# Gated loads in groups, and layer 1 of one stripe chunk by chunk, in a fused attention and feed-forward kernel

## The chip, the cores and the metric

The kernel runs on one core of a Trainium2 chip. The metric is device time in microseconds (us) of one execution, as a median over executions. All times compared here are of the fast state of the machine, unless a run is said to be slow.

Engines: TensorE (PE in the profile; PEld are its weight loads), VectorE (DVE), ScalarE (ACT), GpSimd (POOL) and SyncE (SP, whose queue issues most DMA). An engine waits for the others by semaphores. In this kernel the program order on each engine is the order in which the Python code emits the work.

## The reference, cut to what matters

The inputs q, k and v have shape (4, 8, 768, 64). A decayed causal linear attention gives 3072 tokens of width 512, which go through a feed-forward layer of width 2048.

```python
# attention: in blocks, with a running state per head
intra = (q_b k_b^T * Dmask) v_b
inter = (q_b * lam_pow) @ kv_state
kv_state = lam_block * kv_state + (k_b * rev_pow)^T v_b
# feed-forward ("smelu" is a smooth ReLU)
h = x @ w_in                       # 3072 x 512 @ 512 x 2048
g = where(h >= 1, h, where(h <= -1, 0, (h + 1)**2 / 4))
out = g @ w_out                    # 2048 x 512
```

## The kernel before: the parts that matter

Tokens come in 24 chunks of 128. Four chunks make a stripe of 512 tokens; there are six stripes. A chunk has two units `u` (half of the heads each), and a unit has three steps:

- `t`: transpose q (`pq`), multiply k by [v, identity] (`pk`); ScalarE copies `pq` to `qbd` and half of `pk` to `kT`; VectorE adds the other half to the state `U`.
- `s`: scores `ps`, masked by VectorE into `sc`.
- `o`: output `po` from `U` and `sc`; ScalarE copies it to `xT`, the input of layer 1.

`cast` scales q and k to bf16 (GpSimd, in the first stripe k by VectorE) and casts v into `vi` (ScalarE). `l1(s, i)` and `l2(s, i)` are steps of layer 1 and layer 2 of stripe `s`, 16 each, four 512-column matmuls per step.

```python
def l1(s, ni):
    ph = pp_h.tile([128, MS], F32, name="ph", tag="ph")
    for ko in range(KO):
        nc.tensor.matmul(ph, lhsT=w_in_sb[:, ko, ni * 128:(ni + 1) * 128], rhs=xT[s][:, ko, :],
                         start=(ko == 0), stop=(ko == KO - 1))
    # ... ScalarE: r = relu(ph + 1); every second step VectorE's three SmeLU instructions t, w, gT

# prologue: attention of stripe 0, weights started from chunk 1 on
ensure_loaded(CPS - 1)                       # CPS = 4
for c in range(CPS):
    ensure_cast(c, nc.vector)
    if c >= 1:
        load_w_in(state["wi"]); state["wi"] += 1
    for _ in range(4):                       # t(u) | s(u) ; o(u-1) comes behind t(u)
        a, b_ = att_step()
        for f in a + b_: f()
load_w_in(state["wi"])
for i in range(WS): load_w_out(i)
ensure_loaded(CPS + 1); ensure_cast(CPS)
# ... one att_step; ensure_loaded(CPS + PF)  with PF = 5

# main loop: in each of 16 steps of a stripe
#   l1(s, i) ; t or s of attention further on ; smelu(s, i) ; l2(s - 1, i) ; o of attention
```

So t always stands before the o of the unit ahead, t and s of one unit are a whole step (l1 and l2) apart, and attention of stripe 1 is spread over layer 1 of stripe 0.

## Time and profile before

The median is 263.86 us (263.35 to 263.87, 3 runs). The profiled execution spans 263.5 us.

| stretch, us | what happens | TensorE busy |
|---|---|---|
| 0 to 28.5 | attention of stripe 0 | 14.85 of 28.5 |
| 28.5 to 41.5 | nearly nothing: waits for chunk 4's v | 0.47 of 13 |
| 41.5 to 79 | attention of stripe 1 and layer 1 of stripe 0 | 28.08 of 37.5 |
| 79 to 240 | layer 1, layer 2 and attention mixed | 160.06 of 161 |

First the page of the kernel before: busy time by engine, then the span in 40 equal slices of 6.6 us. A digit is a busy share in tenths; PEclk is the granted TensorE clock in tenths.

```profile
span 263.5 us, 3576 instructions
PE 222.8 (85%) x1209; PEld 118.7 (45%) x1232; DVE 143.8 (55%) x245; ACT 173.7 (66%) x389; POOL 54.2 (21%) x61
...
PE   0567306666889999999999999999999999999993
...
PEclk9999755999999999999999999999999999999998
```

The stretches of the table, from the view by windows (length, busy time of each engine with its count, granted clock, DMA share, GB/s):

```profile
core 0: us, PE busy (x) PEld busy (x) DVE busy (x) ACT busy (x) POOL busy (x), PEclk, DMA share, GB/s
0.00:28.50 28.50, 14.85 (x72) 8.19 (x73) 13.53 (x28) 18.90 (x46) 12.56 (x22) 0.96 1.08 188
28.50:41.50 13.00, 0.47 (x4) 0.26 (x2) 0.74 (x2) 1.10 (x3) 1.04 (x1) 0.63 1.22 196
41.50:79.00 37.50, 28.08 (x159) 15.29 (x162) 26.21 (x39) 29.77 (x71) 15.75 (x14) 0.93 1.22 217
79.00:240.00 161.00, 160.06 (x892) 86.30 (x908) 99.17 (x172) 118.58 (x262) 24.87 (x24) 1.00 0.31 74
```

The hole at 28.5 us in the view of waits (28 to 42 us): TensorE waits for ScalarE's v cast, and that cast for a DMA. The eight weight loads had been issued by then and shared the DMA engines, which moved 196 GB/s all through the hole.

```profile
PE pk L173 <- ACT vi_152 L158: 12.6, 1, 12.6
ACT vi_152 L158 <- DMA vf<-in_v_dram: 11.9, 1, 11.9
```

### The profile page before, as it was taken

What the parts mean: (1) busy time and instruction counts of PE and PEld (TensorE: products, weight loads), DVE (VectorE), ACT (ScalarE), POOL (GpSimd) and SP (SyncE); (2) the same over time, 40 slices, a digit from 0 to 9 for tenths busy, and PEclk for the clock granted to TensorE, in tenths of its full rate; (3) what the DMA queues carried; (4) which work ended last, traced back from release to release, by engine and by line L of the source; (5) the groups of instructions that cost most, each with busy time, mean ns of one, the idle gap of its engine ahead of it and who ended that gap; (6) DMA issues with size and microseconds to landing.
All of it is one profiled execution on the core that took longest, in us unless ns stands there. A gap on an engine that the chain in (4) does not pass through costs nothing.

```text
span 263.5 us, 3576 instructions
## 1 busy us (share of the span) xinstructions
PE 222.8 (85%) x1209; PEld 118.7 (45%) x1232; DVE 143.8 (55%) x245; ACT 173.7 (66%) x389; POOL 54.2 (21%) x61
## 2 busy tenths in 40 slices
PE   0567306666889999999999999999999999999993
PEld 0234203333445555555555555555555544444441
DVE  3554201388887576657574766574747645555300
ACT  4768303778996977797779777977796754554210
POOL 3418111552340332033303320333000000000000
PEclk9999755999999999999999999999999999999998
DMA  6999999999990526753574357110111011111122
GB/s 134 210 217 187 196 196 220 210 226 218 218 202 2 138 67 120 159 128 85 108 159 121 88 113 163 40 40 0 42 41 40 2 40 40 40 42 40 40 80 80
DMA packets 82721, 29.58 MB, mean 112 GB/s; under 512 B 75536, under 2 KB 79632, under 8 KB 82704
## 3 DMA queue, kind: packets, MB, share of 16 engines
q1 hardware_dynamic: 78480, 25.18, 45.5%
q0 software_dynamic: 4224, 4.19, 9.7%
q8 instruction: 9, 0.15, 0.3%
q14 instruction: 8, 0.07, 0.1%
HBM read 27.27 MB, written 6.29 MB: 127 GB/s over the span
## 4 chain that ended last, share of the span: by engine, by line
PE 69%; DVE 3%; ACT 1%; issue 0%; ACTq 0%
PE py L258 31%; PE ph L234 26%; PE po L207 3%; PE ps L192 3%; PE pk L173 2%; PE po L206 2%; PE pq L169 1%; DVE gT L250 1%; DVE w_726 L249 1%; DVE sc L195 0%; DVE w_768 L249 0%; ACT r L238 0%; DVE U L186 0%; ACT xT L212 0%; ACT osb L262 0%
## 5 line engine op out<-in xcount | busy, mean ns | idle before, releaser
L234 PE MATMUL ph<-xT,w_in_sb 128*128 128x512 bf16 x380 | 99.6, 383 | 1.7 <-ACT r L238 1.3
L238 ACT ACTIVATE r<-ph,one 128x512 bf16<-128x512 f32 x96 | 65.9, 687 | 43.3 <-PE ph L234 39.6
L258 PE MATMUL py<-w_out_sb,gT 128*128 128x512 bf16 x365 | 92.3, 379 | 1.0
L234 PEld LDWEIGHTS <-w_in_sb 128*128 128x128 bf16 x384 | 37.9, 99 | 37.6 <-issue 2.8
L258 PEld LDWEIGHTS <-gT 128*128 128x128 bf16 x384 | 37.6, 98 | 32.3
L153 POOL TENSOR_TENSOR qs<-qf,tab_q 128x512 bf16<-128x512 f32 x24 | 25.3, 1052 | 121.7 <-PE pq L169 92.0
L186 DVE TENSOR_TENSOR U<-pk,U 128x256 bf16<-128x256 f32 x32 | 13.6, 424 | 56.5 <-ACT kT L179 56.5
L212 ACT CAST xT<-po 64x256 bf16<-64x256 f32 x96 | 35.3, 367 | 4.5 <-PE po L207 3.7
L195 DVE TENSOR_TENSOR sc<-ps,causal 128x512 bf16<-128x512 f32 x48 | 32.9, 685 | 4.6 <-PE ps L192 4.0
L156 POOL TENSOR_TENSOR ks<-kf,tab_k 128x512 bf16<-128x512 f32 x20 | 22.3, 1117 | 7.9 <-DMA kf<-in_k_dram 7.9
L262 ACT COPY osb<-py 128x512 f32<-128x512 f32 x24 | 14.2, 591 | 12.4 <-PE py L258 12.4
L169 PE MATMUL pq<-ident,qs 128*128 128x128 bf16 x96 | 14.3, 235 | 6.7 <-POOL qs L153 6.7
L179 ACT CAST kT<-pk 128x256 bf16<-128x256 f32 x48 | 17.9, 372 | 2.4 <-PE pk L173 1.3
L173 PE MATMUL pk<-vi_152,ks 128*128 128x256 bf16 x32 | 6.8, 298 | 14.6 <-ACT vi_152 L158 12.6
L169 PEld LDWEIGHTS <-qs 128*128 128x128 bf16 x96 | 10.1, 106 | 16.8 <-POOL qs L153 6.7
L173 PEld LDWEIGHTS <-ks 128*128 128x128 bf16 x96 | 8.1, 103 | 20.5 <-issue 8.1
L192 PEld LDWEIGHTS <-kT 128*128 128x128 bf16 x96 | 8.5, 101 | 19.4 <-ACT kT L179 11.0
L158 ACT CAST vi_152<-vf 128x512 bf16<-128x512 f32 x8 | 4.9, 610 | 11.9 <-DMA vf<-in_v_dram 11.9
L177 ACT COPY qbd_146<-pq 64x256 bf16<-64x256 bf16 x32 | 11.6, 361 | 1.6 <-PE pq L169 1.2
L177 ACT COPY qbd_144<-pq 64x256 bf16<-64x256 bf16 x32 | 11.5, 361 | 0.6 <-PE pq L169 0.2
L177 ACT COPY qbd_148<-pq 64x256 bf16<-64x256 bf16 x32 | 11.5, 361 | 0.5
L206 PEld LDWEIGHTS <-U 128*128 128x128 bf16 x80 | 8.2, 102 | 7.8 <-issue 3.7
(187 smaller groups left out, 213.9 us busy)
## 6 DMA issues: line engine op xcount, KB each, us to landing
qf<-in_q_dram SPq DMA_DIRECT2D x24, 256.0 KB, 4.8
kf<-in_k_dram SPq DMA_DIRECT2D x24, 256.0 KB, 4.7
vf<-in_v_dram SPq DMA_DIRECT2D x24, 256.0 KB, 5.0
out_dram<-osb SPq DMA_DIRECT2D x24, 256.0 KB, 2.0
w_in_sb<-in_moe_w_in_dram POOLq DMA_DIRECT2D x4, 512.0 KB, 8.7
w_out_sb<-in_moe_w_out_dram POOLq DMA_DIRECT2D x4, 512.0 KB, 15.5
lam_b<-in_lam_dram SPq DMA_DIRECT2D x1, 4.0 KB, 2.9
```

Source lines behind the costliest of these rows:

```text
L153: nc.gpsimd.tensor_tensor(t, qf, _bc(tab_q[:, cb, :], 2, D), op=AX.mult)
L156: k_eng.tensor_tensor(t, kf, _bc(tab_k[:, cb, :], 2, D), op=AX.mult)
L169: nc.tensor.transpose(out=pq[:, j, :], in_=qs[c][:, 2 * hp:2 * hp + 2, :].rearrange("p a d -> p (a d)"), identity=ident)
L173: nc.tensor.matmul(pk[:, j], lhsT=ks[c][:, 2 * hp:2 * hp + 2, :].rearrange("p a d -> p (a d)"), rhs=vi[c % NV][:, hp], start=True, stop=True)
L177: nc.scalar.copy(out=qb[hi * 64:hi * 64 + 64, :, hi, :], in_=pq[hi * 64:hi * 64 + 64])
L179: nc.scalar.copy(out=t, in_=pk[:, :, 1, :])
L192: nc.tensor.matmul(ps[:, 2 * j:2 * j + 2, :], lhsT=kT[u][:, j, :], rhs=qbd[u % NQ][:, j], start=True, stop=True)
L195: nc.vector.tensor_tensor(t, ps, _bc(causal, 1, 4), op=AX.mult)
L212: nc.scalar.copy(out=xT[st][hi * 64:hi * 64 + 64, 2 * hf:2 * hf + 2, off:off + C], in_=po[hi * 64:hi * 64 + 64, :, hi, :])
L234: nc.tensor.matmul(ph, lhsT=w_in_sb[:, ko, ni * 128:(ni + 1) * 128], rhs=xT[s][:, ko, :], start=(ko == 0), stop=(ko == KO - 1))
L238: nc.scalar.activation(out=r_t[s][:, ni % 2, :], in_=ph, func=AF.Relu, bias=one[:, 0:1])
L258: nc.tensor.matmul(py, lhsT=gT[s][:, ko, ms * 128:(ms + 1) * 128], rhs=w_out_sb[:, ko, :], start=(ko == 0), stop=(ko == FO - 1))
```

## The change

The intent: bring in the data strictly in the order in which it is needed, so that no weight delays a token chunk that is needed earlier, and give TensorE work from layer 1 of stripe 1 (a quarter as soon as a chunk is done) while layer 2 still lacks its weights. In `items`, the first `t` of a chunk now stands behind the last `o` of the chunk ahead, where it stood before it. The diff, cut to its core:

```diff
-    def load(c):
+    def load(c, after=None):          # the first DMA of the chunk waits for the DMA `after`
...
+    nc.scalar.preload_act_table_set("natural_log_exp_and_others")
-    nc.sync.dma_start(out=lam_b, ...)
+    nc.scalar.dma_start(out=lam_b, ...)
-    NV = 3                            # and qkp bufs 3
+    NV = 4                            # and qkp bufs 4
...
+    def l1(s, ni, n, part):           # n = 1: as before; n = 4: 4 x 4 matmuls of 128 columns,
+        ...                           # one quarter (one chunk) of the stripe, 4 row blocks of w_in
...
+    items = []
+    for u in range(NU):
+        if u % 2 == 0 and u > 0:
+            items += [("o", u - 1), ("t", u)]        # next chunk only after the last o
+        else:
+            items += [("t", u)] + ([("o", u - 1)] if u > 0 else [])
+        items.append(("s", u))
...
+    load_to(CPS - 1)
+    for c in range(CPS):
+        cast_to(c)
+        if c == CPS - 1:
+            for i in range(WS):
+                load_w_in(i)
+            load_to(CPS, after=w_dma[2])
+            load_to(2 * CPS - 1)
+        att_to(done(c))
+    run(zip_(l1s(0, 1, 0), []), 0)                   # layer 1 of stripe 0, alone
+    att_to(done(CPS))                                # chunk 4, alone
+    for c in range(CPS + 1, 2 * CPS):                # chunks 5, 6, 7, each with a quarter
+        run(zip_(l1s(1, CPS, c - CPS - 1), []), done(c) - st["it"])
+    for i in range(WS):
+        load_w_out(i)
+    load_to(2 * CPS, after=w_dma[WS + 2])
+    load_to(2 * CPS + LD - 1)
+    st["ahead"] = True
+    run(zip_(l1s(1, CPS, CPS - 1), []), 0)           # the last quarter
+    run(zip_([], l2s(0)), done(3 * CPS - 1) - st["it"])     # layer 2 of stripe 0 with attention
+    for s in range(2, NST + 1):                      # l1, items, smelu, l2, items: spread evenly
+        a = done(min((s + 2) * CPS, NCH) - 1)
+        run(zip_(l1s(s, 1, 0) if s < NST else [], l2s(s - 1)), a - st["it"])
```

More of the change, by code (lines that the diff above doesn't have):

```diff
@@ L55 @@
     NU = NCH * 2
+    LD = 6
     const = ctx.enter_context(tc.tile_pool(name="const", bufs=1))
     big = ctx.enter_context(tc.tile_pool(name="big", bufs=1))
-    ld = ctx.enter_context(tc.tile_pool(name="ld", bufs=6))
-    qkp = ctx.enter_context(tc.tile_pool(name="qkp", bufs=3))
+    ld = ctx.enter_context(tc.tile_pool(name="ld", bufs=LD))
+    qkp = ctx.enter_context(tc.tile_pool(name="qkp", bufs=4))
     ktp = ctx.enter_context(tc.tile_pool(name="ktp", bufs=3))
@@ L79 @@
     qkv_ld = {}
-    def load(c):
+    w_dma = []
+    SYNC = mybir.DependencyInfo(mybir.DependencyClass.Sync, mybir.DependencyReason.DATA)
+    def load(c, after=None):
         b, s0 = c // NCB, (c % NCB) * C
@@ L85, in load @@
             t = ld.tile([128, H, D], F32, name=f"{name}f", tag=f"{name}f")
-            nc.sync.dma_start(out=t, in_=src[b, :, s0:s0 + C, :].rearrange("h p d -> p h d"))
+            d = nc.sync.dma_start(out=t, in_=src[b, :, s0:s0 + C, :].rearrange("h p d -> p h d"))
+            if after is not None:
+                tc.add_manual_dep(d.ins, after.ins.name, SYNC)
+                after = None
             ts.append(t)
         qkv_ld[c] = ts
+    nc.scalar.preload_act_table_set("natural_log_exp_and_others")
     lam_b = const.tile([128, H], F32)
-    nc.sync.dma_start(out=lam_b, in_=lam.partition_broadcast(128))
+    nc.scalar.dma_start(out=lam_b, in_=lam.partition_broadcast(128))
     load(0)
@@ L139, in load_w_in, with cast @@
         n = d_ff // WS
-        nc.gpsimd.dma_start(out=w_in_sb[:, :, i * n:(i + 1) * n], in_=w_in_r[:, :, i * n:(i + 1) * n])
+        w_dma.append(nc.gpsimd.dma_start(out=w_in_sb[:, :, i * n:(i + 1) * n],
+                                         in_=w_in_r[:, :, i * n:(i + 1) * n]))
     def load_w_out(i):
         n = FO // WS
-        nc.gpsimd.dma_start(out=w_out_sb[:, i * n:(i + 1) * n, :], in_=w_out_r[:, i * n:(i + 1) * n, :])
+        w_dma.append(nc.gpsimd.dma_start(out=w_out_sb[:, i * n:(i + 1) * n, :],
+                                         in_=w_out_r[:, i * n:(i + 1) * n, :]))
     qs, ks = {}, {}
-    def cast(c, k_eng):
+    def cast(c):
         qf, kf, vf = qkv_ld.pop(c)
@@ L155, in cast @@
         t = qkp.tile([128, H, D], BF16, name="ks", tag="ks")
-        k_eng.tensor_tensor(t, kf, _bc(tab_k[:, cb, :], 2, D), op=AX.mult)
+        (nc.vector if c < CPS else nc.gpsimd).tensor_tensor(t, kf, _bc(tab_k[:, cb, :], 2, D), op=AX.mult)
         ks[c] = t
@@ L200, in stage_o @@
         cb = c % NCB
-        st, off = c // CPS, (c % CPS) * C
+        sx, off = c // CPS, (c % CPS) * C
         po = pp_o.tile([128, 2, 2, 128], F32, name="po", tag="po")
@@ L208, in stage_o, with smelu @@
                              start=(cb == 0), stop=True)
-        if st not in xT:
-            xT[st] = xp.tile([128, KO, MS], BF16, name="xT", tag="xT")
+        if sx not in xT:
+            xT[sx] = xp.tile([128, KO, MS], BF16, name="xT", tag="xT")
         for hi in range(2):
-            nc.scalar.copy(out=xT[st][hi * 64:hi * 64 + 64, 2 * hf:2 * hf + 2, off:off + C],
+            nc.scalar.copy(out=xT[sx][hi * 64:hi * 64 + 64, 2 * hf:2 * hf + 2, off:off + C],
                            in_=po[hi * 64:hi * 64 + 64, :, hi, :])
-    def att(i):
-        u, odd = i // 2, i % 2
-        a, b_ = [], []
-        if not odd:
-            if u < NU:
-                a.append(lambda: stage_t(u))
-            if 1 <= u <= NU:
-                b_.append(lambda: stage_o(u - 1))
-        elif u < NU:
-            a.append(lambda: stage_s(u))
-        return a, b_
     gT, r_t, py_t = {}, {}, {}
-    def l1(s, ni):
+    def l1(s, ni, n, part):
         ph = pp_h.tile([128, MS], F32, name="ph", tag="ph")
-        for ko in range(KO):
-            nc.tensor.matmul(ph, lhsT=w_in_sb[:, ko, ni * 128:(ni + 1) * 128], rhs=xT[s][:, ko, :],
-                             start=(ko == 0), stop=(ko == KO - 1))
-        if ni % 2 == 0:
+        m = MS // n
+        for j in range(n):
+            for ko in range(KO):
+                nc.tensor.matmul(ph[:, j * m:(j + 1) * m],
+                                 lhsT=w_in_sb[:, ko, (ni + j) * 128:(ni + j + 1) * 128],
+                                 rhs=xT[s][:, ko, part * m:(part + 1) * m],
+                                 start=(ko == 0), stop=(ko == KO - 1))
+        i = (ni // n) % 2
+        if i == 0:
             r_t[s] = rp.tile([128, 2, MS], BF16, name="r", tag="r")
-        nc.scalar.activation(out=r_t[s][:, ni % 2, :], in_=ph, func=AF.Relu, bias=one[:, 0:1])
-    def smelu(s, ni):
-        if ni % 2 == 0:
+        nc.scalar.activation(out=r_t[s][:, i, :], in_=ph, func=AF.Relu, bias=one[:, 0:1])
+    def smelu(s, ni, n, part):
+        if (ni // n) % 2 == 0:
             return
+        m = MS // n
         r = r_t[s]
-        if ni == 1:
+        if s not in gT:
             gT[s] = gp.tile([128, FO, MS], BF16, name="gT", tag="gT")
@@ L249, in smelu @@
         nc.vector.tensor_tensor(w, r, t, op=AX.subtract)
-        nc.vector.tensor_tensor(gT[s][:, ni - 1:ni + 1, :], w, t, op=AX.mult)
+        nc.vector.tensor_tensor(
+            gT[s][:, ni - n:ni + n, part * m:(part + 1) * m],
+            w.rearrange("p a (b m) -> p (a b) m", m=m), t.rearrange("p a (b m) -> p (a b) m", m=m), op=AX.mult)
     def l2(s, i):
@@ L264, in l2 @@
             nc.sync.dma_start(out=out[m0:m0 + 128, :], in_=o)
-    PF = 5
-    state = {"ld": 2, "cast": 0, "att": 0, "wi": 0, "wo": 0}
-    def ensure_loaded(c):
-        while state["ld"] <= min(c, NCH - 1):
-            load(state["ld"])
-            state["ld"] += 1
-    def ensure_cast(c, k_eng=None):
-        while state["cast"] <= min(c, NCH - 1):
-            cast(state["cast"], k_eng or nc.gpsimd)
-            state["cast"] += 1
-    def att_step():
-        a, b_ = att(state["att"])
-        state["att"] += 1
-        return a, b_
@@ L285 @@
-    NSUB = 2 * NU + 1
-    ensure_loaded(CPS - 1)
-    for c in range(CPS):
-        ensure_cast(c, nc.vector)
-        if c >= 1:
-            load_w_in(state["wi"])
-            state["wi"] += 1
-        for _ in range(4):
-            a, b_ = att_step()
-            for f in a + b_:
-                f()
-    load_w_in(state["wi"])
+    items = []
[5 more added lines that the diff above has]
+        items.append(("s", u))
@@ new lines, with att_to @@
+    items.append(("o", NU - 1))
+    pos_of = {it: i for i, it in enumerate(items)}
+    fns = {"t": stage_t, "s": stage_s, "o": stage_o}
+    st = {"it": 0, "cast": 0, "ld": 2, "ahead": False}
+    def att_to(n):
+        while st["it"] < min(n, len(items)):
+            kind, u = items[st["it"]]
+            if kind == "t" and u % 2 == 0:
+                cast_to(u // 2)
+            fns[kind](u)
+            if kind == "s" and u % 2 == 1 and st["ahead"]:
+                cast_to(u // 2 + 1)
+            st["it"] += 1
@@ new lines, in cast_to, with load_to, done, run @@
+    def cast_to(c):
+        while st["cast"] <= min(c, NCH - 1):
+            cast(st["cast"])
+            st["cast"] += 1
+            if st["ahead"]:
+                load_to(st["cast"] - 1 + LD)
+    def load_to(c, after=None):
+        while st["ld"] <= min(c, NCH - 1):
+            load(st["ld"], after)
+            st["ld"] += 1
+    def done(c):
+        return pos_of[("o", 2 * c + 1)] + 1
+    def run(steps, n_att):
+        a0, ns = st["it"], len(steps)
+        for i, (f1, f2) in enumerate(steps):
+            if f1 is not None:
+                l1(*f1)
+            att_to(a0 + (n_att * (2 * i + 1)) // (2 * ns))
+            if f1 is not None:
+                smelu(*f1)
+            if f2 is not None:
+                l2(*f2)
+            att_to(a0 + (n_att * (2 * i + 2)) // (2 * ns))
@@ new lines, in l1s, with l2s, zip_ @@
+    def l1s(s, n, part):
+        return [(s, ni, n, part) for ni in range(0, FO, n)]
+    def l2s(s):
+        return [(s, i) for i in range(FO)]
+    def zip_(a, b):
+        n = max(len(a), len(b))
+        return list(zip(a + [None] * (n - len(a)), b + [None] * (n - len(b))))
+    load_to(CPS - 1)
+    for c in range(CPS):
+        cast_to(c)
[5 more added lines that the diff above has]
+        att_to(done(c))
@@ L299 @@
+    run(zip_(l1s(0, 1, 0), []), 0)
+    att_to(done(CPS))
+    for c in range(CPS + 1, 2 * CPS):
+        run(zip_(l1s(1, CPS, c - CPS - 1), []), done(c) - st["it"])
     for i in range(WS):
         load_w_out(i)
-    ensure_loaded(CPS + 1)
-    ensure_cast(CPS)
-    a, b_ = att_step()
-    for f in a + b_:
-        f()
-    ensure_loaded(CPS + PF)
-    def target(g):
-        base = 4 * CPS + 1
-        if g < 16:
-            return base + (18 * (g + 1)) // 16
-        return min(NSUB, base + 18 + (g - 15))
@@ L315 @@
-    for s in range(NST + 1):
-        for i in range(FO):
-            g = s * FO + i
-            todo_a, todo_b = [], []
-            while state["att"] < min(NSUB, target(g)):
-                c = state["att"] // 4
-                ensure_loaded(c + PF)
-                ensure_cast(c + 1)
-                a, b_ = att_step()
-                todo_a += a
-                todo_b += b_
-            if s < NST:
-                l1(s, i)
-            for f in todo_a:
-                f()
-            if s < NST:
-                smelu(s, i)
-            if s > 0:
-                l2(s - 1, i)
-            for f in todo_b:
-                f()
+    load_to(2 * CPS, after=w_dma[WS + 2])
```

## The prediction

> **What bounds it now.** Two regimes. From about 79 us on, TensorE is the limit: the table of windows shows it 99% busy from 80 to 240 us, and the chain of waits is an unbroken run of L1 and L2 groups (four 512-column matmuls per 0.86 us), four steps with two attention units in 8.87 us. Before that it is far from full: by the timeline, attention of chunks 0 to 3 runs to 28 us, then all engines stand from 28.5 to 41.5 us because chunk 4's k and v loads queue behind eight weight loads (k and v land 11 and 17 us after their issue; TensorE waits 12.6 us for the v cast). Then ScalarE nearly fills 50 to 79 us (8.1 to 9.6 us of each 10).
>
> **What changes.** Removed: the 13 us load stall, and a table load of 1.28 us. The weights landed at about 196 GB/s from 30 to 40 us and a token chunk takes 3.4 us to issue, so by estimate chunk 3 lands near 17 us, w_in near 30, chunk 7 near 43, w_out near 58, before use: loads stop being the limit.
>
> Added: serial order. A chunk's first unit follows the previous chunk's last o: ScalarE's v cast (0.61) stands behind two xT copies (0.74). The trace's durations, walked through that order:
> - unit change inside a chunk 2.1 us, between chunks 4.4 to 4.9 (was 3.3 to 3.9): stripe 0's attention ends near 34 us instead of 28.
> - L1 of stripe 0 alone: 13.8 us of matmuls, about 2 more for a cold start; to 51 us. The Trainium skill ("TensorE: Matmul & The Clock Gate", Part 1) says the clock halves when TensorE has been idle; the trace agrees (256-column matmuls 0.21 us apart until 22 us, 0.11 later). VectorE's SmeLU ends near 54.
> - chunk 4's attention alone, behind that: to 58.
> - chunks 5, 6, 7, each with a quarter of L1: serial chain L1 group, ReLU 0.69, v cast 0.61, qbd 0.75, kT 0.37, ..., xT 0.74; 9.2 us each, ScalarE busy 7.6 of it: to 86. The last quarter: to 90.
>
> So L2 starts near 90 us, with L1 of two stripes and 8 chunks done; 169.6 us of TensorE work remain (10 of 13.8, 16 chunks at 1.98). In before, 168.5 us remain at 91 us (end of work at 259.5). No gain by then.
>
> After that the order costs more: s now follows t with one L1 group between (1.2 us of TensorE, 1.5 needed by qbd and kT copies), so about 0.4 us stall per two units, 5 us over three stages; in the L2-only stage nothing stands between them: 1.2 us, four times, 5 us. Tail 4 us.
>
> **Predicted:** 90 + 170 + 10 + 4 = about 273 us, 3.5% slower; range 262 to 283. Faster by over 2%: 0.12; within 2%: 0.24; slower: 0.64.
>
> **What would show it.** Right: no DMA wait above 2 us after 10 us; first L2 matmul at 84 to 96 us; TensorE waits for kT (s) and vi (pk) of 10 us or more in sum after the first L2; 20 to 80 us at about half TensorE use. Wrong: first L2 before 80 us, or steady stages of 35.5 us.
>
> **What would make it wrong.** Quarters that overlap better (7.6 us) and a quicker stripe 0 give a first L2 near 78 and 260 us; a cold clock in the quarters, or 128-column matmuls at over 80 ns, 280.

## The result, and the profile after

The changed kernel takes 284.94 us (283.5 to 286.4, 4 runs), the kernel before 263.87 us in the same rounds. The traced execution is the slowest of the four (286.4 us), 1.5 us above the median, so its phases are in sum that much longer than those of a median run. The ratio is 1.080 (95% interval 1.074 to 1.086). A ratio here is the mean time of one kernel's fast runs over that of the other's of the same rounds, so it is not quite the ratio of the medians. Executions over 1.5% slower than the fastest of the same kernel are left out of the means.

The page after: TensorE's row and clock row show two dips instead of one hole, and a long stretch at lowered clock in the middle.

```profile
span 284.7 us, 3965 instructions
PE 239.9 (84%) x1424; PEld 132.4 (46%) x1424; DVE 150.8 (53%) x246; ACT 177.4 (62%) x388; POOL 61.6 (22%) x61
...
PE   0566899368747888779999999999999999999994
...
PEclk9999999757798799999999999999999999999999
```

The phases of the new program, again by windows:

```profile
0.00:33.60 33.60, 17.91 (x77) 8.70 (x77) 14.56 (x30) 18.20 (x46) 10.54 (x19) 1.00 1.09 187
33.60:60.40 26.80, 20.58 (x87) 8.99 (x86) 19.34 (x28) 15.69 (x29) 9.93 (x11) 0.88 1.00 177
60.40:93.90 33.50, 23.56 (x248) 20.80 (x248) 19.26 (x28) 20.13 (x45) 8.75 (x8) 0.79 0.75 142
93.90:99.00 5.10, 5.08 (x62) 5.08 (x62) 2.13 (x4) 2.06 (x3) 0.00 (x0) 0.67 0.02 3
99.00:126.30 27.30, 22.56 (x149) 13.03 (x146) 9.82 (x18) 18.91 (x47) 8.16 (x8) 1.00 0.61 146
126.30:238.50 112.20, 108.45 (x619) 57.14 (x617) 69.88 (x115) 85.78 (x193) 24.21 (x16) 1.00 0.24 66
```

| phase | predicted | measured |
|---|---|---|
| attention of stripe 0 ends | 34 us | 33.6 us |
| layer 1 of stripe 0 ends | 51 us | 50.4 us |
| chunk 4 alone ends | 58 us | 60.4 us |
| chunks 5, 6, 7 with a quarter each | 9.2 us each, to 86 | 11.5, 10.9, 11.1 us, to 93.9 |
| last quarter, first layer 2 matmul | 90 us | 99.0 us |
| layer 2 of stripe 0 with attention | 21.7 + 5 us | 27.3 us |
| three full stages (layer 1, layer 2, attention) | 35.5 + 1.7 us each | 37.6, 37.1, 37.5 us |

The hole of 13 us is gone, and TensorE waits for no DMA after it. But the work between was put in series. In the timeline of TensorE (start, length, instruction, in brackets the wait before it) a chunk change in stripe 0 looks like this: 12.69 to 14.38 us, TensorE has the transposed q and waits for the v cast.

```profile
12.69 0.42 PE L178 MATMUL pq<-ident,qs 128*128 128x128 bf16 x2
14.38 0.59 PE L182 MATMUL pk<-vi_153,ks 128*128 128x256 bf16 x2 [1.26 <-ACT vi_153 L167]
```

ScalarE's timeline tells why. The cast stands behind the xT copies of the o ahead, which is now emitted first:

```profile
12.94 0.74 ACT L221 CAST xT<-po 64x256 bf16<-64x256 f32 x2 [1.28 <-PE po L216]
13.71 0.62 ACT L167 CAST vi_153<-vf 128x512 bf16<-128x512 f32 x1
```

The Trainium skill ("TensorE: Matmul & The Clock Gate", Part 1, on queue depths) says that ScalarE and VectorE queues are strictly first in, first out. These lines agree: v had landed at about 10.7 us, and its cast ran only 0.03 us after the copies ended at 13.68.

A quarter on TensorE (the second, 71.93 to 82.78 us) and VectorE in the same time:

```profile
71.93 0.94 PE L233 MATMUL ph<-xT,w_in_sb 128*128 128x128 bf16 x14 [0.72 <-ACT xT L221]
...
74.15 0.43 PE L182 MATMUL pk<-vi_155,ks 128*128 128x256 bf16 x2 [1.17 <-ACT vi_155 L167]
74.37 1.91 PE L233 MATMUL ph<-xT,w_in_sb 128*128 128x128 bf16 x16
...
78.56 1.06 PE L233 MATMUL ph<-xT,w_in_sb 128*128 128x128 bf16 x16
...
81.55 0.39 PE L216 MATMUL po<-sc,vi_155 128*128 128x256 bf16 x2 [1.72 <-DVE sc L204]
```

```profile
77.36 1.03 DVE L250 TENSOR_SCALAR t_802<-r 128x1024 bf16<-128x1024 bf16 x1
78.42 1.42 DVE L252 TENSOR_TENSOR w_804<-r,t_802 128x1024 bf16<-128x1024 bf16 x1
79.87 0.69 DVE L253 TENSOR_TENSOR gT<-w_804,t_802 128x1024 bf16<-128x1024 bf16 x1
80.48 0.42 DVE L193 CAST U<-pk 128x256 bf16<-128x256 f32 x1
80.81 0.68 DVE L204 TENSOR_TENSOR sc<-ps,causal 128x512 bf16<-128x512 f32 x1
```

Three things are to be seen. TensorE waits three times within one quarter (for xT, the v cast, sc). The same 16 matmuls of 128 columns take 1.91 us at 74 us and 1.06 us at 79 us: the clock had halved. And VectorE's t and w took 1.03 and 1.42 us, where they took 0.42 and 0.69 us at 81 us, so sc came late.

Later, in layer 2 of stripe 0, nothing but t stands between t and s of every second unit, and TensorE idles until kT is copied:

```profile
106.72 0.38 PE L182 MATMUL pk<-vi_153,ks 128*128 128x256 bf16 x2
108.30 0.39 PE L201 MATMUL ps<-qbd_145,kT 128*128 128x256 bf16 x2 [1.19 <-ACT kT L188]
```

### The profile page after: what moved, and what is told of

The parts are those of the page before. It is cut to its first block, busy times and chain, and to the rows that moved or that the text cites. A ratio compares the mean times of both kernels' runs of the same rounds, so it can differ in the third digit from the quotient of the medians.

```text
span 284.7 us, 3965 instructions
## 1 busy us (share of the span) xinstructions
PE 239.9 (84%) x1424; PEld 132.4 (46%) x1424; DVE 150.8 (53%) x246; ACT 177.4 (62%) x388; POOL 61.6 (22%) x61
## 5 line engine op out<-in xcount | busy, mean ns | idle before, releaser
L233 PE MATMUL ph<-xT,w_in_sb 128*128 128x512 bf16 (+1 forms) x576 | 105.6, 329 | 5.6 <-ACT xT L221 4.9
L263 PE MATMUL py<-w_out_sb,gT 128*128 128x512 bf16 x384 | 95.9, 379 | 0.0
L233 PEld LDWEIGHTS <-w_in_sb 128*128 128x128 bf16 x576 | 52.8, 108 | 36.9 <-issue 10.9
L162 POOL TENSOR_TENSOR qs<-qf,tab_q 128x512 bf16<-128x512 f32 x24 | 29.5, 1227 | 136.2 <-PE pq L178 92.8
L263 PEld LDWEIGHTS <-gT 128*128 128x128 bf16 x384 | 37.5, 98 | 36.8
L204 DVE TENSOR_TENSOR sc<-ps,causal 128x512 bf16<-128x512 f32 x48 | 33.1, 690 | 36.9 <-PE ps L201 36.3
L195 DVE TENSOR_TENSOR U<-pk,U 128x256 bf16<-128x256 f32 x32 | 13.5, 421 | 39.6 <-ACT kT L188 39.6
L165 POOL TENSOR_TENSOR ks<-kf,tab_k 128x512 bf16<-128x512 f32 x20 | 25.4, 1271 | 1.0 <-DMA kf<-in_k_dram 0.8
L178 PE MATMUL pq<-ident,qs 128*128 128x128 bf16 x96 | 14.9, 242 | 6.1 <-POOL qs L162 6.1
L201 PEld LDWEIGHTS <-kT 128*128 128x128 bf16 x96 | 7.5, 103 | 23.5 <-ACT kT L188 20.4
L186 ACT COPY qbd_149<-pq 64x256 bf16<-64x256 bf16 x32 | 11.7, 366 | 9.1 <-PE pq L178 8.5
L186 ACT COPY qbd_147<-pq 64x256 bf16<-64x256 bf16 x32 | 11.7, 366 | 8.4 <-PE pq L178 8.0
L186 ACT COPY qbd_145<-pq 64x256 bf16<-64x256 bf16 x32 | 11.7, 366 | 8.2 <-PE pq L178 7.8
L182 PEld LDWEIGHTS <-ks 128*128 128x128 bf16 x96 | 8.7, 108 | 14.1 <-issue 12.1
L201 PE MATMUL ps<-qbd_145,kT 128*128 128x256 bf16 x32 | 7.3, 318 | 3.0 <-ACT kT L188 3.0
L182 PE MATMUL pk<-vi_151,ks 128*128 128x256 bf16 x24 | 5.2, 305 | 5.4 <-ACT vi_151 L167 2.7
## 6 DMA issues: line engine op xcount, KB each, us to landing
qf<-in_q_dram SPq DMA_DIRECT2D x24, 256.0 KB, 4.6
kf<-in_k_dram SPq DMA_DIRECT2D x24, 256.0 KB, 4.9
vf<-in_v_dram SPq DMA_DIRECT2D x24, 256.0 KB, 4.4
out_dram<-osb SPq DMA_DIRECT2D x24, 256.0 KB, 2.0
```

The source lines that it names most:

```text
L162: nc.gpsimd.tensor_tensor(t, qf, _bc(tab_q[:, cb, :], 2, D), op=AX.mult)
L165: (nc.vector if c < CPS else nc.gpsimd).tensor_tensor(t, kf, _bc(tab_k[:, cb, :], 2, D), op=AX.mult)
L178: nc.tensor.transpose(out=pq[:, j, :], in_=qs[c][:, 2 * hp:2 * hp + 2, :].rearrange("p a d -> p (a d)"), identity=ident)
L186: nc.scalar.copy(out=qb[hi * 64:hi * 64 + 64, :, hi, :], in_=pq[hi * 64:hi * 64 + 64])
L201: nc.tensor.matmul(ps[:, 2 * j:2 * j + 2, :], lhsT=kT[u][:, j, :], rhs=qbd[u % NQ][:, j], start=True, stop=True)
L204: nc.vector.tensor_tensor(t, ps, _bc(causal, 1, 4), op=AX.mult)
```

## Experiments

Eleven kernels ran; all gave correct results. "First L2" is the start of the first layer 2 matmul in the profile; it is 79.1 us in the kernel before and 99.0 in the changed one.

| run | median, us | ratio to before (95%) | first L2, us |
|---|---|---|---|
| order_only | 286.22 | 1.089 (1.081 to 1.096) | 98.4 |
| loads_only | 262.77 | 0.997 (0.991 to 1.003) | 76.5 |
| loads_nowait | 254.84 | 0.967 (0.962 to 0.972) | 68.6 |
| t_first | 269.5 | 1.024 (1.018 to 1.031) | 88.3 |
| whole_l1 | 283.91 | 1.075 (1.069 to 1.081) | 96.8 |
| warm | 281.67 | 1.066 (1.060 to 1.072) | 94.4 |
| pool_quiet | 287.45 | 1.087 (1.080 to 1.094) | 94.5 |
| warm_quiet | 283.42 | 1.075 (1.072 to 1.078) | 89.8 |
| interleave | 256.01 | 0.970 (0.965 to 0.975) | 63.1 |
| best | 252.7 (6 fast runs) | 0.961 (0.958 to 0.964) | slow profile |
| best_nogate | 253.38 | 0.961 (0.957 to 0.965) | 59.9 |

### Which half of the change costs: order_only, loads_only, loads_nowait

order_only is the changed kernel with the loads of the kernel before:

```diff
-        if c == CPS - 1:
-            for i in range(WS):
-                load_w_in(i)
-            load_to(CPS, after=w_dma[2])
-            load_to(2 * CPS - 1)
+        if c >= 1:
+            load_w_in(c - 1)
         att_to(done(c))
+    load_w_in(CPS - 1)
+    for i in range(WS):
+        load_w_out(i)
+    load_to(CPS + 5)
...
-    for i in range(WS):
-        load_w_out(i)
-    load_to(2 * CPS, after=w_dma[WS + 2])
```

> The changed kernel's order of work with the loads of the kernel before (weights from chunk 1 on, no gates). Theory A: chunk 4 is not used before 50 us, so its late landing at 34 to 41 us hurts nobody: 281 to 288 us, the same as the changed kernel within 2%. Rival B (the gates cause the loss): it comes back toward 264 us.

Measured: 286.22 us, first L2 at 98.4 us. In this order of work the loads make no difference clear of noise (the intervals, 1.081 to 1.096 and 1.074 to 1.086, overlap): the late chunk 4 is hidden, and the early one would not be used earlier. The loss is in the order of work.

loads_only is the kernel before with the changed kernel's loads (the same gates; w_out is issued behind GpSimd's casts of chunk 7, as in the changed kernel):

```diff
-            load(state["ld"])
+            c_ = state["ld"]
+            load(c_, after=w_dma[2] if c_ == CPS else w_dma[WS + 2] if c_ == 2 * CPS else None)
...
+            if state["cast"] == 2 * CPS:
+                for i in range(WS):
+                    load_w_out(i)
...
-        if c >= 1:
-            load_w_in(state["wi"])
+        if c == CPS - 1:
+            for i in range(WS):
+                load_w_in(i)
```

> The kernel before, with its own order of work, but the changed kernel's order of loads, gates included (4 chunks, w_in, 4 chunks, w_out). Theory A (the loss is the new order of work; the loads by themselves are good): the stall of 13 us at 28.5 us shrinks to about 5 us, because chunk 4 now lands near 33 us; first L2 matmul near 71 instead of 79 us; time 253 to 258 us. Rival B (gating the loads costs: idle DMA at each gate, later data): time at or above 264 us.

Measured: 262.77 us, the same as before within the interval. Both theories missed. The first hole did shrink to 5.5 us, but a second one opened: the order of the kernel before uses chunk 8 before it uses w_out, and the gate puts chunk 8 behind w_out. By the view of waits from 56 to 68 us:

```profile
POOL qs L158 <- DMA qf<-in_q_dram: 14.0, 2, 12.6
...
PE ps L197 <- ACT kT L184: 8.0, 2, 7.6
...
ACT vi L163 <- DMA vf<-in_v_dram: 6.6, 1, 6.6
```

kT is late because ScalarE stands at the v cast of chunk 8, ahead of it in its queue. So "in order of need" is a property of a list of loads and an order of work together; for this order of work the list was wrong in two places.

loads_nowait is the same order of issue with no gate (`load(c_)` without `after`).

> As the run with the loads alone, but no group waits for the one ahead: chunks 4 to 7 are issued straight after chunk 3 beside w_in. Theory A: chunk 4 is there at 28 us, no stall, first L2 near 66 us, 249 to 254 us, that is 2 to 5 us better than with the gates. If the gate is what protects the order, it is worse than the gated run.

Measured: 254.84 us, 3.3% faster than the kernel before, without any change to the order of work. A hole of 6 us is left: chunk 5's v lands at 37 us, beside w_in, and a ReLU stands behind its cast on ScalarE.

```profile
37.24 0.62 ACT L163 CAST vi<-vf 128x512 bf16<-128x512 f32 x1 [7.11 <-DMA vf<-in_v_dram]
37.88 1.27 ACT L243 ACTIVATE r<-ph,one 128x512 bf16<-128x512 f32 x2
```

### Which part of the order of work: t_first, whole_l1

t_first undoes one rule of the changed kernel:

```diff
-        if u % 2 == 0 and u > 0:
+        if u in (2 * CPS, 4 * CPS):
             items += [("o", u - 1), ("t", u)]
```

> The changed kernel with one ordering rule undone: t of the next chunk (and the v cast that goes with it) again stands before o of the last unit, except at the two stripe borders 4 and 8. Theory A (serial order at chunk changes and t directly before s): stripe 0's attention ends at 29 to 30 us instead of 33.6, each quarter about 1 us shorter, steady stages back from 37.9 to 35.5 us and the L2-only stage from 28.6 to about 23: in all 262 to 268 us. If the quarters and the cold clock are the whole loss, it gains under 5 us.

Measured: 269.5 us, a little above the range expected. That is 15.4 us less than the changed kernel (284.94). First L2 came 10.7 us earlier (88.3 against 99.0): layer 1 of stripe 0 starts at 28.4 instead of 33.6 us, and the second and third quarters take 8.1 us (from 66.98 to 75.12 and to 83.23) instead of 10.9 and 11.1. The time from the first to the last layer 2 matmul fell from 181.3 to 175.0 us. Full stages are 35.7, 36.1 and 36.5 us, so part of the stage loss is left; TensorE's only waits there are for xT at the stripe borders (up to 0.9 us each).

The rule does not act through the longer chain alone. With it undone, the three quarters ran at a granted clock of 0.97, where the changed kernel shows 0.79, so part of the gain is the clock:

```profile
58.00:83.20 25.20, 18.18 (x244) 16.30 (x244) 17.78 (x28) 18.01 (x41) 8.53 (x8) 0.97 1.16 212
```

It is also not the only cost: interleave, below, which adds to t_first only that layer 1 and the chunks are no longer worked in series, takes another 13.5 us (269.5 to 256.01). So the loss has two parts of similar size, this rule and the series of phases.

whole_l1 drops the quarters:

```diff
-    for c in range(CPS + 1, 2 * CPS):
-        run(zip_(l1s(1, CPS, c - CPS - 1), []), done(c) - st["it"])
+    att_to(done(2 * CPS - 1))
...
-    run(zip_(l1s(1, CPS, CPS - 1), []), 0)
+    run(zip_(l1s(1, 1, 0), []), 0)
```

> The changed kernel without the chunk by chunk part: attention of chunks 4 to 7 alone, then layer 1 of stripe 1 whole, with 512-column matmuls. If the quarters hide work as intended, this is 10 us or more slower (14 us of layer 1 laid bare). If the quarters only stretch the serial chain (theory A: 11.1 us each against about 7 for a chunk alone), the first L2 comes at 60.4 + 3 x 7 + 15.5 = about 97 us instead of 99.0 and the time is 280 to 286 us, within 2% of the changed kernel.

Measured: 283.91 us, first L2 at 96.8 us, 2.2 us earlier than with the quarters. The quarters hide nothing in this order: chunks 5 to 7 alone end at 80.05 us, 6.5 us each, and layer 1 takes 17 us behind them; with the quarters it is 38.6 us for the same work (60.4 to 99.0). The windows show that TensorE has half its clock while chunks stand alone:

```profile
72.00:83.00 11.00, 8.05 (x29) 3.60 (x30) 2.86 (x5) 5.71 (x14) 2.21 (x3) 0.50 1.23 199
```

### What the blind walk of the quarters left out: warm, pool_quiet, warm_quiet

The walk gave 90 us for the first L2, it was 99. Two suspects are visible in the trace of the quarters: the clock and VectorE's stretched instructions.

warm fills TensorE's idle time in chunks 4 to 7 with matmuls into a PSUM tile (an accumulator of TensorE) that nobody reads:

```diff
+    def fill(n):
+        d = pp_y.tile([128, d_model], F32, name="py", tag="py")
+        for i in range(n):
+            nc.tensor.matmul(d, lhsT=ident, rhs=w_in_sb[:, 0, 0:512], start=True, stop=True)
...  in stage_t, before the pk matmuls:
+        if CPS <= c < 2 * CPS and hf == 0:
+            fill(3)
...  in stage_o, before the po matmuls:
+        if CPS <= c < 2 * CPS and hf == 1:
+            fill(4)
```

> The changed kernel with idle TensorE time in chunks 4 to 7 filled by 7 unused 512-column matmuls per chunk (3 before the pk matmuls of the first unit, 4 before the po matmuls of the second). If the half clock stretches the quarters, the granted clock between 60 and 94 us rises from 0.62 to 0.84 toward 1, the quarters shrink from 11.1 to about 10 us, and the time falls by 3 to 6 us to 279 to 282. If the serial chain over ScalarE and VectorE is all, no gain: 284 to 287.

Measured: 281.67 us, first L2 at 94.4 us. The granted clock from 60 to 94 us rose from between 0.69 and 0.85 to between 0.90 and 0.98 (over thirds of that time), the quarters took 9.5, 9.7 and 10.7 us, the last one 3.6 instead of 5.1. Doing useless work made the kernel 3.3 us faster (difference of the medians, from different rounds; the ratios, 1.066 and 1.080, have intervals that do not meet), so the clock is part of the loss.

pool_quiet holds GpSimd's casts of chunk 8 and all later ones back until the first matmuls of the last quarter:

```diff
-        nc.gpsimd.tensor_tensor(t, qf, _bc(tab_q[:, cb, :], 2, D), op=AX.mult)
+        g = nc.gpsimd.tensor_tensor(t, qf, _bc(tab_q[:, cb, :], 2, D), op=AX.mult)
+        if c == 2 * CPS:
+            tc.add_manual_dep(g.ins, marks[FO + FO - FO // CPS].ins.name, SYNC)
```

> The changed kernel with GpSimd's casts of chunks 8 and later held back until the first matmuls of the last quarter, so that GpSimd is idle while VectorE does SmeLU in the quarters. If VectorE's stretched instructions there (t 1.03 instead of 0.42 us, w 1.42 instead of 0.69) come from GpSimd, they go back to 0.42 and 0.69, and quarters 2 and 3 become about 1.3 us shorter each; time 282 to 284 us, since the first is less affected. If not, nothing changes.

Measured: VectorE's instructions in the second quarter went back as expected,

```profile
76.87 0.42 DVE L254 TENSOR_SCALAR t<-r 128x1024 bf16<-128x1024 bf16 x1
77.32 0.69 DVE L256 TENSOR_TENSOR w<-r,t 128x1024 bf16<-128x1024 bf16 x1
```

the quarters took 12.1, 8.4 and 10.1 us and the first L2 came at 94.5 us. Not all of this is VectorE: the clock shifted too. By windows the quarters had a granted clock of 0.64, 1.00 and 0.83 (0.69, 0.84 and 0.85 in the changed kernel), and the last quarter took 3.5 us at 1.00 instead of 5.1 at 0.67. In the third quarter, where the clocks are nearly the same, the gain is 1.1 us. The total still was 287.45 us. The held casts then ran from 92 to 103 us beside SmeLU (t 0.82 and 1.26, w and gT 1.41 us), layer 2 of stripe 0 took 33.1 us instead of 27.3, and layer 2 from its first to its last matmul 187.0 us instead of 181.3. The expectation of the total was wrong because it left out where the casts would go.

The Trainium skill ("SBUF — State Buffer", Terms) says that VectorE and GpSimd share a pair of SBUF ports, held for a whole instruction, and that the loser blocks fully. The runs agree in kind: with GpSimd idle the stretched times are gone, in the same place of the program.

warm_quiet has both edits.

> The changed kernel with both earlier interventions: filler matmuls in chunks 4 to 7 and GpSimd's casts of chunks 8 and later held back to the last quarter. If the half clock and GpSimd's hold on VectorE are what the blind walk of 90 us left out, the first L2 matmul comes at 89 to 92 us (changed kernel 99.0; each alone 94.4); the total still loses the late casts after that, 279 to 283 us. If they overlap in what they save, it stays at 93 or 94 us.

Measured: the first L2 at 89.8 us; the quarters took 8.7, 8.4 and 8.7 us, the last 3.6. Each alone gives 94.4 and 94.5. By windows (the three quarters, then the last one):

```profile
60.40:86.20 25.80, 21.78 (x265) 17.84 (x269) 15.62 (x28) 19.50 (x45) 0.00 (x0) 1.00 0.90 168
86.20:89.80 3.60, 3.55 (x62) 3.49 (x62) 1.40 (x3) 2.02 (x4) 2.46 (x3) 1.00 0.07 15
```

So the clock and GpSimd's hold on VectorE together account for the 9.2 us by which the first L2 was later than it need have been. How they share it is less sure. Against warm, whose clock was already 0.90 to 0.98, the quiet GpSimd takes off 4.6 us. But these are single traces, and where a stretch of half clock falls differs between them: in order_only, with the same order of work as the changed kernel, the last quarter took 3.6 us at a clock of 1.00, not 5.1. The total, 283.42 us, was a little above the 279 to 283 expected.

### A version that beats both: interleave, best, best_nogate

interleave keeps the changed kernel's loads, takes t_first, and puts the chunks of stripe 1 back over layer 1 of stripe 0, and layer 1 of stripe 1 over layer 2 of stripe 0:

```diff
-    run(zip_(l1s(0, 1, 0), []), 0)
-    att_to(done(CPS))
-    for c in range(CPS + 1, 2 * CPS):
-        run(zip_(l1s(1, CPS, c - CPS - 1), []), done(c) - st["it"])
+    run(zip_(l1s(0, 1, 0), []), done(2 * CPS - 1) - st["it"])
...
-    run(zip_(l1s(1, CPS, CPS - 1), []), 0)
-    run(zip_([], l2s(0)), done(3 * CPS - 1) - st["it"])
-    for s in range(2, NST + 1):
+    for s in range(1, NST + 1):
```

> The changed kernel's loads, with t before o as in t_first and attention of chunks 4 to 7 spread over the 16 steps of layer 1 of stripe 0, and layer 1 of stripe 1 over layer 2 of stripe 0. Theory A: first L2 at 62 to 68 us instead of 99, steady stages 35.5 us, time 249 to 256 us, faster than the kernel before. If the load gates bind, it waits for chunk 4 until 34 us and chunk 8 until 62 us and lands near 258.

Measured: 256.01 us, 3.0% faster than before. TensorE still waits for chunk 4 early in layer 1, first for the cast q, then for the cast v:

```profile
32.77 0.40 PE L178 MATMUL pq<-ident,qs 128*128 128x128 bf16 x2 [2.98 <-POOL qs L162]
34.62 0.59 PE L182 MATMUL pk<-vi,ks 128*128 128x256 bf16 x2 [1.46 <-ACT vi L167]
```

best cuts the groups of loads where this order of work needs them: five chunks, w_in, four chunks, w_out, the rest.

```diff
-    load_to(CPS - 1)
+    load_to(CPS)
...
-            load_to(CPS, after=w_dma[2])
-            load_to(2 * CPS - 1)
+            load_to(CPS + 1, after=w_dma[2])
+            load_to(2 * CPS)
...
-    load_to(2 * CPS, after=w_dma[WS + 2])
+    load_to(2 * CPS + 1, after=w_dma[WS + 2])
```

> As interleave, with the groups of loads cut where this order of work first needs them: 5 chunks, w_in, 4 chunks (5 to 8), w_out, the rest; gates kept. Theory A: the TensorE wait of 4.5 us for chunk 4 at 30 to 34.6 us goes, chunk 8 is there when stripe 1's layer 1 starts; first L2 at 57 to 60 us instead of 63, time 249 to 253 us. If w_in then comes too late for layer 1 (it shares the DMA engines with chunk 4), no gain over 256 us.

Measured: 252.7 us over six fast runs (252.86 with the slow one), 3.9% faster than before. It is the lowest median of all, but its interval overlaps those of best_nogate and of loads_nowait (0.962 to 0.972): most of the gain is had by the order of loads alone, without any change to the order of work. Its profiled execution fell in the slow state (258.09 us, left out of the ratio), so no phase is read from it.

best_nogate is best without the two `after` arguments.

> The same order without the two gates. If the gates protect the group ahead, w_in (beside chunks 5 and 6) lands several us later and layer 1 of stripe 0 waits: 1 to 3% slower than best. If order of issue is all that matters: within 1% of best.

Measured: 253.38 us, the same ratio as best. With the groups cut rightly, the order of issue is what counts; that the gates add anything is not shown. The wait for chunk 4 is down to the chain that every chunk has:

```profile
31.49 0.38 PE L182 MATMUL pk<-vi,ks 128*128 128x256 bf16 x2 [1.17 <-ACT vi L167]
```

## Why the prediction was right or wrong

The measured 284.94 us lies outside the range of 262 to 283, by 2 us, and the loss was 8.0% instead of 3.5%. The direction (slower by over 2%, given 0.64) was right.

- **What bounds the kernel before, and the removed stall**: right. The stall of 13 us went, and loads_nowait shows that removing it is worth 3.3% when the order of work is left alone.
- **"Serial order" takes the gain away**: right. order_only keeps the loss without the loads, t_first takes back 15.4 us with one rule, interleave another 13.5 by overlapping the phases.
- **Stripe 0's attention to 34 us, layer 1 to 51 us**: right to within 0.6 us.
- **Chunk 4 alone to 58 us**: 60.4, short by 2.4 us. VectorE's SmeLU of stripe 0 ended at 55.7 us where the walk had 54, and TensorE waited 2.7 us for the state U behind it (until 56.1 us). From there chunk 4 ran at half clock (its po matmuls of 256 columns stood 0.21 us apart).
- **"Chunks 5, 6, 7 ... 9.2 us each" and "the last quarter: to 90"**: this is the step that failed. They took 11.5, 10.9 and 11.1 us and then 5.1, so the first L2 came at 99.0 instead of 90 us. The chain of instructions was the right one, but two of its durations were taken from places with other conditions: full clock for the matmuls, and an unhindered VectorE. The prediction named a cold clock only as a risk, with 280 us. warm_quiet removes both conditions and gives 89.8 us; 25.8 us for three quarters where the walk had 28, which makes up for the later start. So that 89.8 meets the walk's 90 so closely is in part luck: two errors of some 2 us cancel.
- **After the first L2**: right. Predicted 170 + 10 + 4 = 184 us; measured 284.7 - 99.0 = 185.7 us. Layer 2 with attention took 27.3 us (26.7), the stages 37.1 to 37.6 (37.2). The cause fits as well. Counted from the starts of the matmuls in the trace (the gap ahead of an s, less the usual spacing), s was late by 0.33 us twelve times in the three full stages, 4.0 us in all (predicted: 0.4 us, 5 in all), and by 1.27 us four times in layer 2 of stripe 0 (predicted: 1.2 us, four times). Another 2.2 us went to waits for xT at the stripe borders, which the prediction did not have.
- **The signs to look for**: the first L2 was put at 84 to 96 us (99.0). "No DMA wait above 2 us" holds for TensorE, ScalarE and VectorE; GpSimd did wait up to 12.4 us for q, with nothing behind it that was due. "Waits for kT and vi of 10 us or more after the first L2" was a poor sign: TensorE's matmul rows show 4.4 us for kT from 99 to 127 us and 1.9 from 127 to 245, the weight-load rows 5.5 and 8.0 (these overlap matmuls). The starts of the matmuls, above, show the stall better. "Half TensorE use from 20 to 80 us" was wrong as a reading of busy time, since a slow clock makes matmuls look busy (45.2 of these 60 us): from 60 to 70 us TensorE was busy for 8.2 of 10 us at a clock of 0.62.

In sum, of the 11.7 us between 273 and 284.7, 9.0 came before the first L2, nearly all in chunks 4 to 7; the other 2.7 came after it (1.7) and from rounding.

## What to carry to other kernels

An order of loads is right only for a given order of work: find for every load the first instruction that stops the in-order engines, and cut the groups there; here five chunks rather than four before the first weights, and chunk 8 before w_out, turned 256.0 into 252.7 us. Spread a producer and its consumer apart with independent work; putting the next chunk's first step behind the last step of the chunk ahead cost about 15 us, part of it through the clock: more than the 13 us hole that the change was made to close. Try the order of loads alone first: it gave 3.3% of the 3.9% that the best version has. When you walk a chain by hand, take each duration under the conditions it will meet: clock after idle time, and which other engine is running then.

## What the Trainium skill lacked or had wrong

- "TensorE: Matmul & The Clock Gate", Back-to-back issue gap, gives about 81 ns per matmul for a sustained stream of weight load and 128-column matmul. In the last quarter 62 such pairs took 3.5 us in pool_quiet, 56 ns each, at full clock. In the changed kernel the same 62 took 5.1 us, 82 ns each, but at a granted clock of 0.67: the mean of two clocks, not a limit of the weight loads.
- The profile's granted clock is not safe early in a run, where the warning in Part 1 of the same page covers only trace events in general: in the changed kernel the window from 0 to 33.6 us shows 1.00, while the 128-column matmuls at 12.69 us and the 256-column ones of that time stood 0.11 and 0.21 us apart, twice the later spacing of 0.055 and 0.11.
- "SBUF — State Buffer", Terms, tells of the port pair shared by VectorE and GpSimd but gives no times for instructions such as these. Here a 1024-element bf16 subtraction on VectorE took 1.42 instead of 0.69 us, the min-and-scale 1.03 instead of 0.42, beside GpSimd's casts, and those took 1.22 us in the quarters and up to 1.58 us later, instead of 1.04.
